# TensorE work in 64x64 tiles in a fused threshold attention and SoLU kernel

## The chip, the cores and the metric

The kernel runs on one core of one Trainium2 chip. Times are device microseconds (us) of one execution; medians are over four or more executions. Ratios are the mean time of one kernel's fast runs over the mean of the other kernel's fast runs of the same rounds, with a 95% interval, so they are not quite the ratio of the medians that stand beside them. A run over 1.5% above the fastest of its kernel is called slow and left out of ratios. The runs fall in five sessions (the changed kernel, e1 to e4, e5 to e8, e9 to e12, e13 to e15), each with runs of the kernel before beside them; its medians differ by up to 4.7 us between sessions, so I do not tell apart runs of different sessions that lie within some 5 us.

Engines are named as in the profile: PE is TensorE (PEld its weight loads), DVE VectorE, ACT ScalarE, POOL GpSimd, SP SyncE, which here issues transfers. A number such as L411 is a line of the kernel that ran.

## The reference

```python
# q, k, v: 8 batches x 8 heads x 576 tokens x 64, float32; tau = 0.02
scores = (1 / sqrt(64)) * q @ k.T
scores = where(scores >= max(scores) - tau, scores, -1e9)
attn   = exp(scores - max(scores));  attn /= sum(attn) + 1e-9
x      = (attn @ v) as (8*576, 8*64) = (4608, 512)        # tokens x (head, dim)
h      = x @ w_in                                         # 512 -> 1024
u      = h * softmax(h)
ln     = (u - mean(u)) / sqrt(var(u) + 1e-6) * g_ln
out    = ln @ w_out                                       # 1024 -> 512
```

`w_in` and `w_out` arrive as 64-bit floats and are converted on the chip in 16 pieces during the first 18 rounds; `g_ln` and the centring of `u` are folded into `w_out`.

## The kernel before

A pair is two heads of one batch, 64 dimensions each, on partitions 0 to 63 and 64 to 127. A round (one pass of the loop) takes one slot of attention: 128 tokens of both heads (a "last" slot holds the 64 left-over tokens of a pair as a block-diagonal query). Beside it the round does a quarter of a token tile of the feed-forward part: two rounds for `h_ps` (q0, q1), two for `o_ps` of the tile before (q2, q3). The whole kernel is software-pipelined by hand: what a round emits is what each engine has in its queue, in that order.

```python
    pairs_free = ["mm0", "mm1", "mm2"]      # three buffers of two PSUM banks: scores, h_ps
    banks_free = ["x0", "x1"]               # two single banks: transposes, pv, o_ps

    def scores(s):                          # 64x128 tiles: one head per row half
        ...
        for h, t, place in todo:
            tag, ps = take("s_ps")
            ...
            for ks in (slice(0, SM), slice(SM, S)):
                nc.tensor.matmul(out=ps[:, ks], lhsT=lhsT, rhs=kT[hh, ks], start=True, stop=True)

    def maxes(s):                           # VectorE: negated max, then nth = tau - max
    def exps(s):                            # ScalarE: Prelu as threshold (frees the banks), Exp with sum
    def normalise(s):
        nc.gpsimd.tensor_scalar(out=sm, in0=sm, scalar1=1e-9, scalar2=None, op0=ALU.add)
        nc.vector.reciprocal(out=sm, in_=sm)
        for x, w in enumerate(d["w"]):
            nc.gpsimd.tensor_scalar(out=w, in0=w, scalar1=d["sm"][:, x : x + 1], ...)
    def blocks(s):                          # VectorE transposes w in 32x32 blocks to T;
        ...                                 # SyncE issues 16 transfers per unit that sort T into wT
    def attend(key):                        # pv: 128x64 tiles, v against wT, five rounds later

    # the order in the loop of rounds
            scores(rnd); maxes(rnd)
            ...                             # attend, transposes, max and product of a token tile
            exps(rnd)
            if rnd - 1 >= 0 and rnd - 1 in live:
                normalise(rnd - 1)
            for job in late.pop(rnd, []):   # Exp of u, bn_stats, the rs chain, the output
                job()
            ...                             # h_ps or o_ps, then blocks(rnd - 1)
```

The loads of a batch are cut in twelve transfers, spread over rounds, on ScalarE's queue; the raw weights and the outputs are issued there too.

Of the kernel before, what the change touches and what calls it, by code (L numbers as in the profile page):

```python
# [20 lines left out]
def kernel(  # L21
# [23 lines left out]

    nc = tc.nc
# [8 lines left out]
    SCALE = 0.125  # L55

    const = ctx.enter_context(tc.tile_pool(name="const", bufs=1))
    loads = ctx.enter_context(tc.tile_pool(name="loads", bufs=2))
    heads = ctx.enter_context(tc.tile_pool(name="heads", bufs=5))
# [7 lines left out]
    mhalf = const.tile([P, 1], F32, name="mhalf")  # L67
    tau_t = const.tile([P, 1], F32, name="tau_t")
# [11 lines left out]
    NQE = 5  # L80
    q_ends = [const.tile([P, P], F32, name=f"q_end{x}") for x in range(NQE)]


    wTs = [const.tile([P, 5, 4, 160], F32, name=f"wT{x}") for x in range(2)]
    v_ends = [const.tile([P, H, D], F32, name=f"v_end{x}") for x in range(2)]

    batches = {}
    pairs = {}
    units = {}
    turned = 0  # L90
# [4 lines left out]
    pairs_free = ["mm0", "mm1", "mm2"]  # L95
    banks_free = ["x0", "x1"]
# [5 lines left out]
    def take_bank(name):  # L102
        tag = banks_free.pop(0)
        return tag, ps_mm.tile([P, 512], F32, tag=tag, name=name)


    def load(b):
        d = {}
        d["ends"] = ends = loads.tile([P, H, D], F32, tag="ends", bufs=1, name="ends")
        for nm in "qk":  # L110
            d[nm] = loads.tile([P, 4, H, D], F32, tag=nm, bufs=1, name=nm)
        d["v"] = loads.tile([P, H, 4, D], F32, tag="v", bufs=2, name="v")
        d["ve"] = v_ends[b % 2]
        batches[b] = d

        sides = (("q", q, slice(0, ST)), ("k", k, slice(ST, P)))
        if b == 0:

            for h in range(H):
                for (nm, src, side), queue in zip(sides, (nc.sync, nc.scalar if h < 2 else nc.sync)):  # L120
                    queue.dma_start(
                        out=d[nm][:, :, h], in_=src[b, h, 0:SM, :].rearrange("(p t) d -> p t d", t=4)
                    )
                    if h == 1:
                        queue.dma_start(
                            out=ends[side], in_=src[b, :, SM:S, :].rearrange("h p d -> p h d")
                        )
                if h == 1:
                    yield
        else:  # L130
            for nm, src, side in sides:
                for t in range(4):
                    nc.scalar.dma_start(
                        out=d[nm][:, t],
                        in_=src[b, :, 0:SM, :].rearrange("h (p t) d -> t p h d", t=4)[t],
                    )
                    if t % 2:
                        yield
                nc.scalar.dma_start(
                    out=ends[side], in_=src[b, :, SM:S, :].rearrange("h p d -> p h d")  # L140
                )
                yield
        queue = nc.scalar if b else nc.sync
        queue.dma_start(
            out=d["v"].rearrange("p h t d -> p h (t d)"),
            in_=v[b, :, 0:SM, :].rearrange("h (p t) d -> p h (t d)", t=4),
        )
        queue.dma_start(
            out=d["ve"][0:ST], in_=v[b, :, SM:S, :].rearrange("h p d -> p h d")
        )  # L150
        yield

    def constants():
# [4 lines left out]
        nc.gpsimd.memset(mhalf, -0.5)  # L158
        nc.gpsimd.memset(lim[:, 0:1], 1151.0)
        nc.gpsimd.memset(lim[:, 1:2], 255.0 * 8388608.0)  # L160
        for t in q_ends:
            nc.gpsimd.memset(t, 0.0)
        for t in v_ends:
            nc.gpsimd.memset(t[ST:P], 0.0)
        for t in wTs:
            nc.gpsimd.memset(t[ST:P, 4], 0.0)
# [11 lines left out]
        tag, g_ps = take_bank("g_ps")  # L178
# [4 lines left out]
        banks_free.append(tag)  # L183
# [12 lines left out]
    def weight_load(x):  # L196
        raw = work.tile([P, 512], I64 if wide else F32, tag=("xh2", "xh3")[x % 2], bufs=1, name="raw")
        nc.scalar.dma_start(out=raw, in_=piece(x)[0])
        raws[x] = dict(raw=raw)

    def weight_a(x):
# [4 lines left out]
        d["em"] = em = work.tile([P, 2, 512], I32, tag="em", bufs=1, name="em")  # L206
        e, m = em[:, 0], em[:, 1]
# [12 lines left out]
    def weight_b(x):  # L220
# [7 lines left out]
        e, m = d["em"][:, 0], d["em"][:, 1]  # L228
# [11 lines left out]
    def center():  # L240
        ones = work.tile([P, P], F32, tag="ob", name="ones")
        nc.vector.memset(ones, 1.0 / DFF)
        tag, mean = take_bank("mean")
        for c in range(NC):
            nc.tensor.matmul(out=mean, lhsT=ones, rhs=w2[:, c], start=c == 0, stop=c == NC - 1)
        for c in range(NC):
            nc.vector.tensor_tensor(out=w2[:, c], in0=w2[:, c], in1=mean, op=ALU.subtract)  # L247
        banks_free.append(tag)


    def prep(i, step):
        b, hp = divmod(i, NP)
        src = batches[b]
        two = slice(2 * hp, 2 * hp + 2)
        d = pairs.setdefault(i, {})
        tag, tp = take_bank("tp_" + "qke"[step])
        banks_free.append(tag)
        if step < 2:
            nm = "qk"[step]
            for t in range(4):  # L260
                nc.tensor.transpose(
                    out=tp[:, P * t : P * t + P], in_=src[nm][:, t, two],
                    identity=ident,
                )
            d[nm + "T"] = heads.tile([P, SM if step == 0 else S], F32, tag=nm + "T", name=nm + "T")
            if step == 0:
                nc.scalar.activation(out=d["qT"], in_=tp, func=AF.Copy, scale=scl)
            else:
                nc.scalar.copy(out=d["kT"][:, 0:SM], in_=tp)
            return  # L270
        nc.tensor.transpose(out=tp[:, 0:P], in_=src["ends"][:, two], identity=ident)
        for hh in (slice(0, D), slice(D, P)):
            nc.vector.tensor_scalar(
                out=q_ends[i % NQE][hh, hh], in0=tp[hh, 0:ST], scalar1=scl[hh], scalar2=None,
                op0=ALU.mult,
            )
        nc.vector.tensor_copy(out=d["kT"][:, SM:S], in_=tp[:, ST : 2 * ST])
        nonlocal turned
        turned += 1
# [3 lines left out]
    for b in range(B):  # L283
        for half in range(2):
            for hp in range(NP):
                for r in range(2 + half):
                    slots.append((b, half, hp, r))


    def tiles_of(half, r):  # L290
        if half == 0:
            return [(0, r, r), (1, r, 2 + r)]
        if r < 2:
            return [(0, 2 + r, r), (1, 2 + r, 3 + r)]
        return [(None, 4, 2)]
# [3 lines left out]
    def scores(s):  # L299
        b, half, hp, r = slots[s]  # L300
        i = b * NP + hp
        d = pairs[i]
        todo = tiles_of(half, r)
        qT, kT = d["qT"], d["kT"]
        made, tags = [], []
        for h, t, place in todo:
            tag, ps = take("s_ps")
            if h is None:
                hh, lhsT = slice(0, P), q_ends[i % NQE]
            else:  # L310
                hh = slice(D * h, D * h + D)
                lhsT = qT[hh, P * t : P * t + P]
            for ks in (slice(0, SM), slice(SM, S)):
                nc.tensor.matmul(out=ps[:, ks], lhsT=lhsT, rhs=kT[hh, ks], start=True, stop=True)  # L314
            made.append((ps, place))
            tags.append(tag)
        live[s] = dict(ps=made, tags=tags)

    def maxes(s):
        d = live[s]  # L320
        n = len(d["ps"])
        nm = small.tile([P, 2], F32, tag="nm", name="nm")
        for x, (ps, _) in enumerate(d["ps"]):
# [3 lines left out]
        nth = small.tile([P, 2], F32, tag="nth", name="nth")  # L327
        nc.vector.tensor_scalar(  # L328
            out=nth[:, 0:n], in0=nm[:, 0:n], scalar1=tau_t, scalar2=None, op0=ALU.add
        )  # L330
        d["nth"] = nth
# [3 lines left out]
    def exps(s):  # L335
        d = live[s]
        sm = small.tile([P, 2], F32, tag="sm", name="sm")
        d["w"] = []
        for x, (ps, _) in enumerate(d["ps"]):
# [6 lines left out]
        pairs_free.extend(d["tags"])  # L346
# [4 lines left out]
        d["sm"] = sm  # L351

    def normalise(s):
        d = live[s]
        n = len(d["w"])
        sm = d["sm"][:, 0:n]
        nc.gpsimd.tensor_scalar(out=sm, in0=sm, scalar1=1e-9, scalar2=None, op0=ALU.add)  # L357
        nc.vector.reciprocal(out=sm, in_=sm)  # L358
        for x, w in enumerate(d["w"]):
            nc.gpsimd.tensor_scalar(  # L360
                out=w, in0=w, scalar1=d["sm"][:, x : x + 1], scalar2=1.0, op0=ALU.mult,
                op1=ALU.mult,
            )

    n_units = 0

    def blocks(s):
        nonlocal n_units
        b, half, hp, r = slots[s]
        n = 4 + half  # L370
        key = (b, half, hp)
        if r == 0:
            units[key] = dict(T=work.tile([P, NB, n, 32], F32, tag="T", name="T"))
        T = units[key]["T"]
        d = live.pop(s)
# [308 lines left out]
```

## Time and profile before

| | before |
|---|---|
| median | 1123.45 us (1121.93 to 1125.1) |
| TensorE busy | 92% |
| VectorE, ScalarE, GpSimd busy | 63%, 52%, 28% |
| first `h_ps` starts, last scores end, end | 100.1, 1043.2, 1123.2 us |

The prediction below reads the page's busy shares, chain and groups. To them belong two more views. The first is the page's row for TensorE's granted clock over the span in 40 slices (9 is 90% or more). The second lists what TensorE waited for between 170 and 1044 us: the instruction that waited, what it waited for, us in total, times, longest.

```profile
PEclk9987799999998999999998999999998999999989
```

```profile
PE s_ps L314 <- ACT w L341: 12.5, 8, 2.6
PE pv L410 <- DMA wT<-T: 6.3, 6, 1.7
PE pv L410 <- ACT ob L517: 5.9, 10, 0.8
```

### The profile page before, as it was taken

The numbers are of one execution on the slowest core, as the hardware profiler recorded it, in microseconds if no ns is written. First come the engines' busy times: TensorE is split into PE (matmuls) and PEld (weight loads), VectorE is DVE, ScalarE is ACT, GpSimd is POOL, SyncE is SP. The second block draws the span as 40 slices with busy tenths as digits, with TensorE's granted clock in tenths as the row PEclk, the third lists the DMA queues.
The fourth block names the chain that finished last, engine by engine and source line by source line (L and its number), as shares of the span: only waits on it lengthen the run. The fifth ranks groups of instructions, "written<-read, shape, count | busy, mean of one in ns | idle before, by whom it ended". The sixth has DMA issues, their size and how long they took to land.

```text
span 1123.2 us, 15118 instructions
## 1 busy us (share of the span) xinstructions
PE 1029.3 (92%) x4817; PEld 555.8 (49%) x4817; DVE 711.3 (63%) x1401; ACT 581.2 (52%) x1170; POOL 309.9 (28%) x647
## 2 busy tenths in 40 slices
PE   6867789899999999999999999999999999999988
PEld 4433445445554555455544555445554555445533
DVE  3878866667656667766656667757656667766331
ACT  4656535555555556554555556555555556554211
POOL 2222212332223222332323222332223222432210
PEclk9987799999998999999998999999998999999989
DMA  7598424863467435763467435762467434444400
GB/s 173 140 188 218 109 53 105 170 143 71 108 144 166 104 82 117 167 147 71 107 150 156 104 82 116 170 144 66 110 144 163 103 85 102 98 103 95 94 10 28
DMA packets 259310, 132.11 MB, mean 118 GB/s; under 512 B 96920, under 2 KB 252576, under 8 KB 259232
## 3 DMA queue, kind: packets, MB, share of 16 engines
q1 hardware_dynamic: 173488, 88.15, 36.1%
q10 hardware_dynamic: 85744, 43.00, 15.4%
q8 instruction: 39, 0.64, 0.3%
q14 instruction: 39, 0.32, 0.1%
HBM read 36.70 MB, written 9.44 MB: 41 GB/s over the span
## 4 chain that ended last, share of the span: by engine, by line
PE 51%; DVE 18%; DMA 12%; ACT 6%; SPq 6%; POOL 3%; issue 3%; ACTq 0%; DVEq 0%
PE o_ps L510 15%; PE h_ps L446 13%; PE pv L410 11%; PE s_ps L314 9%; SPq L385 6%; DVE nm L324 5%; DVE T L377 5%; DMA wT<-T 5%; ACT w L341 3%; POOL w L360 3%; DMA v<-in_v_dram 3%; DVE u L465 2%; ACT w L348 2%; DMA q<-in_q_dram 1%; PE tp_u L497 1%
## 5 line engine op out<-in xcount | busy, mean ns | idle before, releaser
L360 POOL TENSOR_SCALAR w<-w,sm 128x576 f32<-128x576 f32 x288 | 211.6, 745 | 562.3 <-DVE sm L358 562.3
L377 DVE STREAM_TRANSPOSE T<-w 128x576 f32<-128x576 f32 x288 | 214.0, 771 | 134.2 <-POOL w L360 100.7
L324 DVE TENSOR_REDUCE nm<-s_ps 128x1 f32<-128x576 f32 x288 | 205.3, 748 | 118.5 <-PE s_ps L314 117.3
L341 ACT ACTIVATE w<-s_ps,nth 128x576 f32<-128x576 f32 x288 | 199.5, 740 | 142.8 <-DVE nth L328 99.0
L510 PE MATMUL o_ps<-w,uT 128*128 128x512 f32 x576 | 263.1, 601 | 5.1 <-DVE w L247 3.5
L314 PE MATMUL s_ps<-kT,qT 64*128 64x512 f32 (+1 forms) x1024 | 218.9, 472 | 39.8 <-ACT w L341 31.6
L446 PE MATMUL h_ps<-w,xh 128*128 128x512 f32 x512 | 239.8, 613 | 0.3 <-ACT w L341 0.3
L348 ACT ACTIVATE w<-w,ntau 128x576 f32<-128x576 f32 x288 | 220.7, 774 | 1.0
L314 PEld LDWEIGHTS s_ps<-kT,qT 64*128 64x128 f32 x1024 | 120.0, 198 | 182.3 <-issue 101.2
L410 PE MATMUL pv<-wT,v 128*64 128x192 f32 (+2 forms) x1536 | 159.2, 348 | 16.6 <-DMA wT<-T 7.0
L510 PEld LDWEIGHTS o_ps<-w,uT 128*128 128x128 f32 x576 | 105.3, 192 | 120.1 <-issue 113.1
L446 PEld LDWEIGHTS h_ps<-w,xh 128*128 128x128 f32 x512 | 95.0, 196 | 104.7 <-issue 103.6
L410 PEld LDWEIGHTS pv<-wT,v 128*64 128x64 f32 x1536 | 108.2, 143 | 44.9 <-issue 19.6
L357 POOL TENSOR_SCALAR sm<-sm 128x2 f32<-128x2 f32 (+1 forms) x160 | 39.0, 243 | 158.5 <-ACT w L348 154.5
L425 ACT COPY xh<-pv 128x256 f32<-128x256 f32 x32 | 11.9, 371 | 108.6 <-PE pv L410 108.6
L497 PE MATMUL tp_u<-ident,u 128*128 128x128 f32 x288 | 45.6, 282 | 13.5 <-ACT ob L517 4.7
L348 ACT ACTIVATION_READ_ACCUMULATOR w<-w,ntau 128x1 f32 x288 | 57.1, 198 | 0.0
L421 ACT COPY xh<-pv 128x256 f32<-128x256 f32 x32 | 11.9, 372 | 86.8 <-PE pv L410 75.0
L410 PE MATMUL pv<-wT,v_end 128*64 128x256 f32 (+2 forms) x384 | 52.8, 336 | 0.0
L459 ACT ACTIVATE u<-h_ps,hm 128x1024 f32<-128x1024 f32 x36 | 39.8, 1105 | 25.1 <-DVE hm L453 25.1
L453 DVE TENSOR_REDUCE hm<-h_ps 128x1 f32<-128x1024 f32 x36 | 43.9, 1219 | 11.9 <-PE h_ps L446 11.7
L500 ACT COPY uT<-tp_u 128x512 f32<-128x512 f32 x36 | 21.0, 585 | 57.7 <-PE tp_u L497 56.0
(65 smaller groups left out, 704.9 us busy)
## 6 DMA issues: line engine op xcount, KB each, us to landing
wT<-T SPq DMA_DIRECT2D x512, 80.0 KB, 2.2
wT<-T SPq DMA_DIRECT2D x256, 100.0 KB, 2.3
wT<-T SPq DMA_DIRECT2D x256, 64.0 KB, 2.1
out_dram<-ob ACTq DMA_DIRECT2D x32, 256.0 KB, 2.6
q<-in_q_dram ACTq DMA_DIRECT2D x28, 256.0 KB, 4.7
k<-in_k_dram ACTq DMA_DIRECT2D x28, 256.0 KB, 4.6
v<-in_v_dram ACTq DMA_DIRECT2D x7, 1024.0 KB, 6.8
raw<-in_moe_w_in_dram ACTq DMA_DIRECT2D x8, 512.0 KB, 4.8
```

The lines of the kernel that those rows point to most:

```text
L314: nc.tensor.matmul(out=ps[:, ks], lhsT=lhsT, rhs=kT[hh, ks], start=True, stop=True)
L324: nc.vector.tensor_reduce(out=nm[:, x : x + 1], in_=ps[:, 0:S], axis=AX.X, op=ALU.max, negate=True)
L341: nc.scalar.activation(out=w, in_=ps[:, 0:S], func=AF.Prelu, bias=d["nth"][:, x : x + 1], scale=1.0, alpha=1.0e30,)
L348: nc.scalar.activation(out=w, in_=w, func=AF.Exp, bias=ntau, scale=1.0, accum_out=sm[:, x : x + 1])
L360: nc.gpsimd.tensor_scalar(out=w, in0=w, scalar1=d["sm"][:, x : x + 1], scalar2=1.0, op0=ALU.mult, op1=ALU.mult,)
L377: nc.vector.transpose(out=T[:, :, place, :], in_=w)
L385: nc.sync.dma_start(out=wT[32 * c : 32 * c + 32, 0:nj, a, 0 : 32 * n], in_=T[32 * a : 32 * a + 32, c : NB : 4].rearrange("p j t q -> p j ( ...
L410: nc.tensor.matmul(out=to[:, a0:a1, 0 : 32 * n], lhsT=vv, rhs=wT[:, c, a0:a1, 32 * first : 32 * first + 32 * n], start=c == 0, stop=c == 4,)
L446: nc.tensor.matmul(out=h[:, f], lhsT=x[:, c], rhs=w1[:, c, f], start=c == 0, stop=c == NP - 1)
L453: nc.vector.tensor_reduce(out=d["nm"], in_=d["h"], axis=AX.X, op=ALU.max, negate=True)
L497: nc.tensor.transpose(out=tp[:, P * c : P * c + P], in_=d["u"][:, x : x + P], identity=ident)
L510: nc.tensor.matmul(out=d["o"], lhsT=d["uT"][:, c], rhs=w2[:, c], start=c == 0, stop=c == NC - 1)
```

## The change

The intent is to make every TensorE instruction in the steady part a 64x64 tile, so that none has to wait at a change of shape until the array has drained, and so that four run at once. To get there the change also

- puts the last tokens of two pairs in one slot (18 slots per batch instead of 20), 
- does the transposes as 64x64 products into the spare columns of the scores' banks, which leaves the scores one pair of buffers (`s0`, `s1`) and `pv`, `h_ps` and `o_ps` another two (`p0`, `p1`),
- sets a GpSimd memset ("fence") between the two parts of a product in which the row halves exchange banks,
- moves `normalise` behind the token tile's `late` jobs, with the reciprocal as a power on GpSimd,
- attends four rounds later instead of five, and moves raw weights and outputs to SyncE's queue and gathers the loads of a batch, still on ScalarE's queue, into ten transfers issued in four rounds.

The core of the diff, with cuts marked; the comments are added here.

```diff
+    def fence(first):
+        m = nc.gpsimd.memset(mark, 0.0)
+        for mm in first:
+            sync(m, mm)
+        return m
...
-        nc.scalar.dma_start(out=raw, in_=piece(x)[0])
+        nc.sync.dma_start(out=raw, in_=piece(x)[0])
...
+    def turn(spare, x, lhsT_of):            # a transpose as four 64x64 products
+        o = spare["base"] + 64 * x
+        to = slice(o, o + 64)
+        for r in range(2):
+            for y in range(2):
+                nc.tensor.matmul(
+                    out=spare[r][ROWS[y], to], lhsT=lhsT_of(r, y), rhs=ident[ROWS[r], ROWS[r]], ...)
...
+    def scores(s, items):
+        ps = [ps_mm.tile([P, 1024], F32, tag=f"s{h}", name="s_ps") for h in range(2)]
+        spare = dict(enumerate(ps), base=S)
+        for n, make, keep in items:         # transposes of q, k, ends or u
+            make(spare, x)
+            ...
+        for ks in (slice(SM, S), slice(0, SM)):
+            for h in range(2):
+                for y in range(2):
+                    ...                     # 64x64 tiles
+        for keep, x in kept:                # ScalarE copies from s0, VectorE from s1
+            keep(spare, x)
...
-        nc.vector.reciprocal(out=sm, in_=sm)
+        nc.gpsimd.tensor_tensor(out=sm, in0=sm, in1=mone, op=ALU.pow)
...
+        for c in range(NP):                 # ff_h; ff_o and attend alike
+            for r in range(2):
+                f = slice(512 * (part ^ r), 512 * (part ^ r) + 512)
+                for y in range(2):
+                    mm = nc.tensor.matmul(
+                        out=h[ROWS[y], f], lhsT=x[ROWS[r], c, ROWS[y]], rhs=w1[ROWS[r], c, f], ...)
+                    if part and not last:
+                        sync(mm, d["fence"])
...
-    LAG_PV = 5
+    LAG_PV = 4
...
-            if rnd - 1 >= 0 and rnd - 1 in live:
-                normalise(rnd - 1)
             for job in late.pop(rnd, []):
                 job()
+            if rnd - 1 in live:
+                normalise(rnd - 1)
```

## The prediction

> **What bounds the kernel now.** I read the busy shares first, then the chain that ended last, then the costliest groups, and last the timeline of TensorE in a few microseconds of the steady part.
>
> ```profile
> PE 1029.3 (92%) x4817; PEld 555.8 (49%) x4817; DVE 711.3 (63%) x1401; ACT 581.2 (52%) x1170; POOL 309.9 (28%) x647
> PE 51%; DVE 18%; DMA 12%; ACT 6%; SPq 6%; POOL 3%; issue 3%; ACTq 0%; DVEq 0%
> L377 DVE STREAM_TRANSPOSE T<-w 128x576 f32<-128x576 f32 x288 | 214.0, 771 | 134.2 <-POOL w L360 100.7
> L324 DVE TENSOR_REDUCE nm<-s_ps 128x1 f32<-128x576 f32 x288 | 205.3, 748 | 118.5 <-PE s_ps L314 117.3
> L341 ACT ACTIVATE w<-s_ps,nth 128x576 f32<-128x576 f32 x288 | 199.5, 740 | 142.8 <-DVE nth L328 99.0
> L360 POOL TENSOR_SCALAR w<-w,sm 128x576 f32<-128x576 f32 x288 | 211.6, 745 | 562.3 <-DVE sm L358 562.3
> L485 POOL TENSOR_TENSOR rs<-rs,mhalf 128x1 f32<-128x1 f32 x36 | 20.4, 567 | 3.0
> ```
>
> TensorE is the bound: 92% busy, first in the chain, and VectorE, next, has 37% to spare. The groups below TensorE wait for it or for each other. So what matters is whether TensorE's busy time is work. The timeline, with start and length in us ahead of each group:
>
> ```profile
> 500.87 1.19 PE L314 MATMUL s_ps<-kT,q_end 128*128 128x512 f32 x4
> ...
> 505.78 0.60 PE L497 MATMUL tp_u<-ident,u 128*128 128x128 f32 x4
> 506.31 1.30 PE L314 MATMUL s_ps<-kT,qT 64*128 64x512 f32 x8
> 507.54 0.33 PE L271 MATMUL tp_e<-ident,ends 128*128 128x128 f32 x1
> ...
> 1050.08 1.52 PE L410 MATMUL pv<-wT,v 128*64 128x192 f32 x16
> ```
>
> Each fp32 product is two matmul records, and one record of N columns streams for 2N cycles: consecutive h_ps records (N = 512) start 428 ns apart, 1024 cycles at 2.4 GHz. Eight 64-row records of two heads take 1.30 us, little more than four full ones (1.19 us): the two row halves **already run side by side**. Likewise sixteen 64-column pv records would need 16 x 160 ns = 2.56 us in series and take 1.52. So tiling has no factor of two left. What it can save is around changes of shape. Records of equal shape follow each other without loss; at a change I find a gap of 0.13 to 0.22 us and a first record 50 to 105 ns longer than its successors. I counted 309 changes (128x128, 64x128, 128x64), gaps under 1 us summing to 47 us; with some 80 ns for each first record, **about 72 us** of the span.
>
> **What the Trainium skill says.** "TensorEngine Tiling (Array Packing)", section Tiling Modes, says a change of tiling mode drains TensorE while tiles of one mode work independently; the gaps and the overlapping heads agree. The same page, Restrictions and Gotchas, says that different row tiles may not use one PSUM bank at once and software must order them: hence the fences; nothing in this trace tests it. "TensorE: Matmul & The Clock Gate", Part 3, gives 10.6 times for 16 concurrent tiles, so four should overlap; the trace shows only two. Its Part 1 says that an idle window of some 3.4 us halves the clock; here the clock falls to half for 6.8 us at 339, 592 and 844 us, so such idle time occurs every two batches.
>
> **The change part by part.** I call one slot of the loop a round; four rounds (two of h_ps, two of o_ps, named q0 to q3) make one token tile.
>
> *TensorE work.* One 64x64 matmul of N columns costs its own tile 4N cycles, and four tiles overlap. Scores: 576 x 4 cycles = 0.96 us per slot as before, but a batch has 18 slots instead of 20, because two pairs' last tokens share one instead of a block-diagonal query being half zeros: 2 x 0.96 = 1.9 us per batch, 15 us in all. h_ps or o_ps: 3.41 us per round, unchanged. A 128x128 transpose costs 107 ns, as 108 now. PV of a unit costs two parts of 5 x 128 x 4 cycles, 1.07 us each, the same sum as before. Instruction count grows about fourfold; where pv had just waited for a semaphore, four TensorE instructions came in 36 ns (494.56 to 494.60 us), so I expect no limit from issue.
>
> A cycle of four rounds is then: q0 and q1 each 0.43 (transposes of u) + 0.96 + 1.07 + 3.41 + 1.07 = 6.94 us; q2 0.43 + 0.96 + 3.41 = 4.80; q3 0.54 + 0.96 + 3.41 = 4.91. Sum **23.6 us**, or 106 us per batch of 4.5 cycles. Before, a batch takes half of 680.0 - 427.3 us (first h_ps two batches apart), 126.4 us. If TensorE never waited, the gain would be 20 us x 8 = 160 us.
>
> *What takes it back.* Scores now have one pair of buffers, s0 and s1, so scores of the next round (and the transposes that share those buffers) must wait until Prelu has read this round's. Also the normalisation on GpSimd is now emitted behind the statistics of the token tile, and its reciprocal is a GpSimd power. Follow q3, with 0 where TensorE has streamed its scores: max starts at 0.2 and takes 1.42 for two, nth until 1.88, u's product (1.22) until 3.1, two bn_stats (1.29) and aggregate (0.21) until 4.6. GpSimd, waiting for it, does four small rs operations (335, 220, 567, 191 ns with 0.09 between) until 6.25, then the sum's add 0.24, power (**my estimate 0.75**, from 567 ns for one column), and the first w (0.745): 8.25. VectorE's in-order queue holds T of the round before: 8.3 to 9.8; a copy of u's transposes (0.42, between 0.22 for 64 columns and 0.67 for 512) until 10.1; only now q0's max, until 11.5; nth 11.7; two Prelus on ScalarE until 13.2; TensorE restarts at 13.4. TensorE, from 0: o_ps 3.41, q0's transposes and scores after q3's Prelu (3.5) until 5.0, then 1.07 + 3.41 + 1.07 until about 10.6. It **stands idle for some 2.8 us**. From 13.4: 0.43 + 0.96 + 1.07 + 3.43 + 1.07 = 20.4, q2 0.43 + 0.96 + 3.43 = 25.2, q3 0.54 + 0.96: **26.8 us** per cycle. Other rounds have slack: q1's Prelu ends at 18.2, before TensorE needs it at 20.4; q2's ends at 25.1 against 25.2.
>
> *Fences.* 127 memsets of about 0.1 us. Each lies 3.4 us or a round ahead of its user, so it should be free; the tightest is q0's PV, behind the delayed normalisation (9.05 against a need at 9.6).
>
> *Other engines.* VectorE loses 196 reciprocals of 0.155 us (30 us) and gains 32 pairs x two copies of 0.42 us (27 us) less 18 us of q_end: near 700 us. GpSimd gains 144 x 0.75 + 36 x 0.57 + 127 x 0.1 = 141 us: about 450. ScalarE loses a little. DMA of w has longer contiguous rows; it is hidden anyway.
>
> *Sum.* Start to the first h_ps: 100.1 us before, bound by VectorE and converting weights; now 12 rounds for 13: 93. Scores end at round 144, so 132 rounds: 32 cycles with h_ps x 26.8 = 858, four rounds without it (no new tile is ready twice) 22, weights still converting in rounds 12 to 16, 6. Tail: from the end of scores the old one takes 80 us (1043 to 1123); the new has 4 h_ps and 5 o_ps tiles of 6.84, transposes and PV 7, output and small waits 13: 82. 93 + 858 + 22 + 6 + 82 = **1061**; I put 1058.
>
> **The rivals.** (a) *TensorE stays the bound and gets nearly all drains back.* If the stall is hidden, as it would be if GpSimd's chain were 2.8 us shorter, 1061 - 32 x 2.8 = 970. For: VectorE's load per cycle is only about 18.5 us of 23.6. Against: the in-order queues above. (b) *VectorE's and GpSimd's latency bounds*, my main case. Each microsecond mis-sized in the chain costs 32 us; a power of 1.2 us makes 1075. (c) *Four small tiles overlap badly, or issue bounds.* The 64-column transposes need an instruction every 13 ns. If weights or issue double PV and transposes, a cycle gains some 6 us: 1240. For: fourfold instructions, and only pairs of tiles are seen overlapping. Against: 64-column score records already follow at 55 ns with two tiles. (d) *Fences held in GpSimd's queue* reach TensorE; one more us each cycle makes 1090.
>
> **Range and chances.** 1058, and 1000 to 1115 eight times in ten: the lower edge is two thirds of the stall hidden, the upper 1.8 us more per cycle. Within 2% needs over 1100.7. Faster 0.80, within 2% 0.12, slower 0.08; the last is rival (c).
>
> **What would show it.** Shape changes gone except in the tail, and 144 slots. Scores' matmuls of four tiles starting within some 40 ns, and h_ps at 3.4 us a part. Waits: TensorE on Prelu (scores' buffers) some 2 to 3 us once a cycle, at u's transposes; VectorE's T waiting for GpSimd's w over 3 us once a cycle; few waits of TensorE on the memset. TensorE's start-to-start of cycles near 26.8 us. I am wrong if cycles are under 25 (stall hidden), or if PV parts take well over 1.1 us each (issue), or if TensorE waits on fences. The least certain terms are the power's length and the overlap of four tiles.

## The result and the profile after

The changed kernel is slower: 1241.53 us median (1236.49 to 1255.22, four runs) against 1123.45 us (1121.93 to 1125.1). The ratio of the fast runs is 1.1036 [1.0998, 1.1074]; the run of 1255.22 us is slow and left out. The prediction said 1058 us and gave slower 0.08.

The page of the changed kernel, which answers to the lines of before: busy shares, clock, and the groups of the chain that the prediction followed. (Its chain of what ended last breaks off at the last instruction and is not read.)

```profile
PE 987.8 (80%) x18569; PEld 684.5 (55%) x18569; DVE 682.3 (55%) x1164; ACT 576.3 (47%) x1241; POOL 442.0 (36%) x930
PEclk7566769898889989899999998999999999999999
L411 ACT ACTIVATE w<-s_ps,nth 128x576 f32<-128x576 f32 x288 | 197.7, 738 | 350.6 <-DVE nth L401 258.1
L439 DVE STREAM_TRANSPOSE T<-w 128x576 f32<-128x576 f32 x288 | 210.7, 764 | 174.7 <-POOL w L427 130.6
L425 POOL TENSOR_TENSOR sm<-sm,mone 128x2 f32<-128x2 f32 x144 | 104.2, 724 | 12.0
```

Busy TensorE time fell by 41.5 us, and VectorE's by 29 us, but the span grew by 111.5 us: no engine is over 80%. ScalarE stands idle 350.6 us in front of Prelu (L411) instead of 142.8. The clock row has a 5 and 6s at the start and more 8s later. What TensorE waited for between 206 and 1144 us:

```profile
PE s_ps L264 <- ACT w L411: 55.8, 64, 4.0
PE h_ps L554 <- ACT ob L673: 30.1, 8, 5.7
PE s_ps L264 <- DVE u L579: 24.7, 24, 3.9
PE o_ps L658 <- ACT xh L520: 10.9, 5, 5.0
PE pv L491 <- POOL mark L106: 5.9, 2, 3.0
```

L264 are the transposes that open a round's use of `s0` and `s1`. They wait 64 times for Prelu, which reads the scores of the round before: that is the wait the prediction named. The second and fourth entries it did not name: ScalarE comes late with an output or a copy of `pv`.

The next four blocks of lines are one stall, the timelines of four engines around the last round of a token tile (q3) and the first of the next (q0). Start and length in us stand ahead; in brackets are the idle time before and what ended it.

TensorE:

```profile
608.68 0.88 PE L264 MATMUL s_ps<-ident,u 64*64 64x64 f32 x30 [0.79 <-DVE u L579]
...
609.40 1.19 PE L385 MATMUL s_ps<-kT,qT 64*64 64x64 f32 x14
...
611.51 3.60 PE L554 MATMUL h_ps<-w,xh 64*64 64x512 f32 x30
...
618.50 0.33 PE L264 MATMUL s_ps<-ident,u 64*64 64x64 f32 x4 [2.29 <-ACT w L411]
...
619.60 2.18 PE L385 MATMUL s_ps<-kT,qT 64*64 64x64 f32 x14
```

VectorE:

```profile
605.72 1.42 DVE L397 TENSOR_REDUCE nm<-s_ps 128x1 f32<-128x576 f32 x2 [0.69 <-ACT qe L335]
...
613.86 1.50 DVE L439 STREAM_TRANSPOSE T<-w 128x576 f32<-128x576 f32 x2 [3.77 <-DMA wT<-T]
615.29 0.38 DVE L617 COPY uT<-s_ps 128x256 f32<-128x256 f32 x1
615.60 1.40 DVE L397 TENSOR_REDUCE nm<-s_ps 128x1 f32<-128x576 f32 x2
```

GpSimd:

```profile
612.26 0.72 POOL L425 TENSOR_TENSOR sm<-sm,mone 128x2 f32<-128x2 f32 x1
613.08 1.48 POOL L427 TENSOR_SCALAR w<-w,sm 128x576 f32<-128x576 f32 x2
```

ScalarE:

```profile
617.71 1.37 ACT L411 ACTIVATE w<-s_ps,nth 128x576 f32<-128x576 f32 x2 [6.48 <-POOL mark L106]
```

Read from the bottom up. TensorE restarts at 618.50, as soon as the first Prelu of 617.71 has read `s0`. Prelu waited for `nth`, and so for q0's max (615.60; the profile names the fence's memset, which ended at about the same time). The max stands in VectorE's queue behind T (613.86), which waited 3.77 us. The profile puts that wait down to a transfer, but T starts when the first of GpSimd's two products, begun at 613.08, is done: that is the power and the delayed normalisation. So far it is the predicted chain, with an idle time of 2.29 us where 2.8 were predicted. Two things are new. q3's max started only at 605.72, some 1.3 us after its scores had streamed, behind two copies out of the score banks and a wait of 0.69 us for ScalarE's copy `qe`. And after the stall fourteen score records take 2.18 us, where those of the round before took 1.19: the clock is at half for some 3.4 us.

To size this I added up, from TensorE's records that start between 180 and 980 us, the gaps under 1 us at changes of shape, all other gaps, and the time at half clock, which costs at most half of itself. A record of N columns is taken to end when its 2N cycles have streamed (428 ns for N = 512, twice that at half clock), so that slow streaming does not count as a gap; gaps count from 20 ns.

| us in 800 | changes of shape, gaps | other gaps | at half clock |
|---|---|---|---|
| before | 246, 34.7 | 59.2 | 23.9 |
| changed | 1, 0 | 143.1 | 94.9 |

The drains are gone, as intended: some 35 us gained. 83.9 us more of other gaps, and up to 35.5 us of clock, took their place.

### The profile page after: what moved, and what is told of

It is laid out like the page before. It is cut to its first block, busy times and chain, and to the rows that moved or that the text cites. A ratio compares the mean times of both kernels' runs of the same rounds, so it can differ in the third digit from the quotient of the medians.

```text
span 1234.7 us, 43204 instructions
## 1 busy us (share of the span) xinstructions
PE 987.8 (80%) x18569; PEld 684.5 (55%) x18569; DVE 682.3 (55%) x1164; ACT 576.3 (47%) x1241; POOL 442.0 (36%) x930
## 5 line engine op out<-in xcount | busy, mean ns | idle before, releaser
L411 ACT ACTIVATE w<-s_ps,nth 128x576 f32<-128x576 f32 x288 | 197.7, 738 | 350.6 <-DVE nth L401 258.1
L554 PE MATMUL h_ps<-w,xh 64*64 64x512 f32 x1856 | 233.6, 623 | 38.0 <-ACT ob L673 30.1
L658 PE MATMUL o_ps<-w,uT 64*64 64x256 f32 x3968 | 233.6, 379 | 11.5 <-ACT xh L520 10.9
L397 DVE TENSOR_REDUCE nm<-s_ps 128x1 f32<-128x576 f32 x288 | 203.9, 749 | 62.2 <-ACT qe L335 24.2
L658 PEld LDWEIGHTS o_ps<-w,uT 64*64 64x64 f32 x3968 | 193.6, 134 | 63.0 <-ACT xh L520 18.9
L491 PEld LDWEIGHTS pv<-wT,v 64*64 64x64 f32 x4096 | 175.6, 143 | 79.6 <-issue 39.8
L491 PE MATMUL pv<-wT,v 64*64 64x128 f32 x4096 | 191.5, 288 | 11.0 <-POOL mark L106 6.9
L385 PE MATMUL s_ps<-kT,qT 64*64 64x64 f32 (+1 forms) x2048 | 184.5, 453 | 19.5 <-ACT w L411 19.1
L554 PEld LDWEIGHTS h_ps<-w,xh 64*64 64x64 f32 x1856 | 106.9, 142 | 118.5 <-issue 68.6
L264 PE MATMUL s_ps<-ident,u 64*64 64x64 f32 x1984 | 63.3, 243 | 83.5 <-ACT w L411 49.5
L264 PEld LDWEIGHTS s_ps<-ident,u 64*64 64x64 f32 x1984 | 51.4, 149 | 107.9 <-ACT w L411 100.3
L425 POOL TENSOR_TENSOR sm<-sm,mone 128x2 f32<-128x2 f32 x144 | 104.2, 724 | 12.0
L385 PEld LDWEIGHTS s_ps<-kT,qT 64*64 64x64 f32 x2048 | 61.2, 148 | 23.3 <-ACT w L411 21.9
L617 DVE COPY uT<-s_ps 128x256 f32<-128x256 f32 x62 | 25.1, 405 | 88.0 <-PE s_ps L385 88.0
L264 PE MATMUL s_ps<-ident,k 64*64 64x64 f32 x992 | 32.0, 239 | 36.1 <-ACT w L411 36.1
```

What stands on the lines that cost most here:

```text
L264: nc.tensor.matmul(out=spare[r][ROWS[y], to], lhsT=lhsT_of(r, y), rhs=ident[ROWS[r], ROWS[r]], start=True, stop=True,)
L385: nc.tensor.matmul(out=ps[h][ROWS[y], ks], lhsT=lhsT, rhs=d["kT"][ROWS[h], ks], start=True, stop=True,)
L397: nc.vector.tensor_reduce(out=nm[:, x : x + 1], in_=ps[:, 0:S], axis=AX.X, op=ALU.max, negate=True)
L411: nc.scalar.activation(out=w, in_=ps[:, 0:S], func=AF.Prelu, bias=d["nth"][:, x : x + 1], scale=1.0, alpha=1.0e30,)
L425: nc.gpsimd.tensor_tensor(out=sm, in0=sm, in1=mone, op=ALU.pow)
L491: mm = nc.tensor.matmul(out=y[ROWS[h], 512 * u : 512 * u + P].rearrange("p (a x) -> p a x", a=4), lhsT=ve[ROWS[r], h0 + h] if j == 4 else ...
```

## The experiments

All are edits of the changed kernel and all gave correct results. I write "loads" for q, k, v of the batches after the first. The runs of before beside them had medians of 1124.8 to 1128.1 us. My theory at first was that the delayed normalisation and ScalarE's queue make the waits; the rivals were the tiling itself, the fences, and SyncE's queue.

**e1_norm_first: the normalisation back ahead of the `late` jobs.**

```diff
+            if rnd - 1 in live:
+                normalise(rnd - 1)
             for job in late.pop(rnd, []):
                 job()
-            if rnd - 1 in live:
-                normalise(rnd - 1)
```

> The normalisation is emitted ahead of the token tile's statistics again, as in the kernel before; nothing else changes. Theory: the 9.9 us round (q3 to q0) is the GpSimd chain of small rs operations ahead of the normalisation, on which VectorE's T and then q0's max wait; T could start 3.7 us earlier, TensorE then waits only for its own work, so 2 to 2.8 us less in each of 33 cycles: about 1165 us (1150 to 1185), and VectorE's wait for GpSimd's w falls from 131 us to under 50. Rival: other waits (ScalarE's blocked queue, u's product) stand right behind and take the time: 1205 to 1240 us.

Measured: 1170.47 us, ratio 1.0401 [1.0343, 1.0459]; 71 us of the 118 are back. The step from q3 to q0 went from 9.9 to 6.5 us in a typical cycle. A step is the time from the first Prelu of a round to that of the next, the median of the steady cycles. The order of one call is the largest single part.

**e2_loads_sp: the loads on SyncE's queue.**

```diff
-                nc.scalar.dma_start(     # q and k
+                nc.sync.dma_start(
...
-                queue = nc.scalar        # ends, and likewise v
+                queue = nc.sync
```

> All loads of later batches are issued by SyncE instead of ScalarE; nothing else changes. Theory: ScalarE stands up to 6 us at a load's issue behind earlier transfers, and holds back the copies that free the buffers of h_ps and o_ps; the waits of h_ps on ob (30 us) and of o_ps on xh (11 us) vanish: about 1200 us. Rival: the load's wait moves to SyncE, delays the transfers of w there, and PV waits instead: within 1% of 1241 us.

Measured: 1207.06 us, ratio 1.0721 [1.0671, 1.0771], 34.5 us less. The changed kernel shows why. ScalarE's timeline (ACTq is the issue of a transfer), and TensorE's:

```profile
671.27 0.40 ACTq L128 DMA_DIRECT2D q<-in_q_dram  x1
...
674.63 0.41 ACTq L128 DMA_DIRECT2D k<-in_k_dram  x1
675.08 0.69 ACT L673 ACTIVATE ob<-o_ps,rs 128x512 f32<-128x512 f32 x1 [2.35 <-DMA wT<-T]
```

```profile
675.82 3.66 PE L554 MATMUL h_ps<-w,xh 64*64 64x512 f32 x32 [1.89 <-ACT ob L673]
```

The issue of k's load waits for almost 3 us in ScalarE's queue; the output `ob` behind it frees the buffer that `h_ps` needs. Before, twelve issues were spread over rounds, and `h_ps` did not share its buffers with `o_ps`.

**e3_norm_loads: both.** The edit is the sum of the two.

> Both edits. Theory: the two waits lie in different rounds and add: some 1120 to 1140 us, and the clock's half-speed stretches in the steady part fall below half of the 27 there were. Rival: the larger of the two alone, 1165 us.

Measured: 1130.57 us, ratio 1.0042 [0.9996, 1.0088]: the same as before. The effects add (71 + 34.5 = 105.5, together 111). With these two moves undone and the tiling kept, the kernel is as fast as before.

**e4_ff128: `h_ps` and `o_ps` in 128x128 tiles, without their fences.**

```diff
-                ff_h(cur, 0, rnd + 1 < NS)
+                ff_h(cur, 0, False)
...
-        if not d["osplit"]:
+        if True:                          # o_ps too, in the same buffer
```

> h_ps and o_ps as 128x128 matmuls without fences, all else in 64x64 tiles. It brings back two changes of shape in each of about 128 rounds and takes away 63 fences. If the drains still counted in full, 128 x 2 x 0.2 = 51 us more: 1290 us. If TensorE is not the bound in most rounds (my theory: it waits some 4 us per cycle), the drains fall partly into its waits: 1245 to 1275 us. If four tiles at once or the fences were the loss (rival c or d), it is faster than 1241 by 20 us or more.

Measured: 1235.88 us, ratio 1.0971 [1.093, 1.1013]. That is below the range of my theory: drains return (200 changes of shape and 29.6 us of gaps between 180 and 980 us), and the time does not move. Other gaps fall from 143.1 to 109.1 us: the drains lie in time in which TensorE would have waited. Its largest wait between 206 and 1144 us is that of the changed kernel; the one for u is smaller (24.7 us there), and that of `h_ps` for `ob` falls from 30.1 to 5.9 us:

```profile
PE s_ps L264 <- ACT w L411: 54.9, 57, 2.6
PE s_ps L264 <- DVE u L579: 16.6, 22, 3.4
```

**e5_weights_act: e3, with the raw weights on ScalarE's queue.**

```diff
-        nc.sync.dma_start(out=raw, in_=piece(x)[0])
+        nc.scalar.dma_start(out=raw, in_=piece(x)[0])
```

> On top of e3: the 16 loads of raw weights are issued by ScalarE again, as in the kernel before. Theory: on SyncE each stood behind 16 issues of w's transfers at 0.6 us, so that VectorE waited 35 us for raw weights, ScalarE 57 us for VectorE, and every second round of the first 16 took 11 to 15 us. The first 18 rounds should take 155 to 165 us instead of 190: 1130 becomes 1095 to 1105 us, later batches unchanged. Rival: the slow start comes from the single pair of score buffers and the conversion itself: 1120 to 1130 us.

Measured: 1095.37 us, ratio 0.9714 [0.9654, 0.9775]; 35 us less, all in the first 18 rounds, which take 152.4 us instead of 190. SyncE is busy for three quarters of the time with the 16 transfers of each unit, as its own timeline of the changed kernel shows (one line is one burst of issues):

```profile
666.02 11.35 SPq L449 DMA_DIRECT2D wT<-T  x16
```

That is 0.71 us per issue; a unit comes every 15 us (nine in a batch of some 137 us), and what is queued behind a burst waits for it. In e3 the first conversion of a piece waits 5.66 us for its raw weights at 46.57 us, and TensorE 9.25 us at 51.48 us behind it.

**e6_copies_early: e5, with the copies out of the score banks ahead of the 512-column scores.** This tests whether the copies can be taken off VectorE's path to max.

```diff
         for ks in (slice(SM, S), slice(0, SM)):
+            if ks.start == 0:
+                for keep, x in kept:
+                    keep(spare, x)
...
-        for keep, x in kept:
-            keep(spare, x)
```

> On top of e5: the copies of the transposes out of the scores' banks are emitted between the 64-column and the 512-column scores instead of after both. Theory: they now wait for the last score matmul and come ahead of max in VectorE's queue, so that each round's chain is 0.4 to 0.7 us longer; beside the 512-column matmuls they should cost nothing: 20 to 35 us less than e5. Rival: TensorE's own 23.6 us per cycle covers them: within 0.5% of e5. Third: TensorE waits for the copies before the 512-column scores: slower than e5 by 20 us or more.

Measured: 1221.98 us, ratio 1.0839 [1.0774, 1.0905], 127 us more than e5. TensorE's waits over the whole run:

```profile
PE s_ps L388 <- ACT qe L335: 64.3, 31, 5.5
PE s_ps L388 <- ACT uT L618: 51.2, 62, 5.5
PE s_ps L388 <- ACT qT L295: 38.4, 31, 6.0
```

The scores now wait for the copies. By the code the two are in different banks of one tile (the 512-column scores fill the first, the copies read the second), so the program orders them by tile; a finer order was not tried. In both orders that were tried the copies cost time: they stand either ahead of max or ahead of the scores.

**e7_lag5: e5, attending five rounds later again.**

```diff
-    LAG_PV = 4
+    LAG_PV = 5
```

> On top of e5: PV follows its last scores by five rounds instead of four. Theory: a 12 us round once or twice per two batches in e3 is PV waiting for w's transfers, delayed on SyncE by the loads; with a round more they have landed: 15 to 30 us less than e5. Rival: the later PV delays the token tiles and the tail by a round or two: within 0.5%, or slower.

Measured: 1080.48 us, ratio 0.9594 [0.9528, 0.9661], 15 us less than e5. `pv` had waited 17.2 us for transfers of wT between 180 and 990 us in e5; in e7 that entry is gone. What TensorE still waits for most, between 180 and 980 us:

```profile
PE s_ps L264 <- DVE u L579: 29.5, 26, 3.8
PE s_ps L264 <- ACT w L411: 11.0, 26, 3.1
```

**e8_loads_pool: e3, with the loads on GpSimd's queue instead of SyncE's.** The edit is e2's with `nc.gpsimd`.

> As e3, but the loads of later batches are issued by GpSimd instead of SyncE. Theory: neither ScalarE nor SyncE is held up; GpSimd has half its time free: 1110 to 1125 us against 1130. Rival: a load that waits for earlier transfers holds up GpSimd's normalisation and fences just as it held up ScalarE: 1145 to 1170 us.

Measured: 1129.25 us, ratio 1.0019 [0.9946, 1.0093], no different from e3 and between the two ranges that I gave. What mattered was that ScalarE was rid of them; whether they stand among SyncE's bursts or apart from them made no measurable difference.

**e9_max_order: the changed kernel, max of `s1` ahead of `s0`**, so that VectorE need not wait at once for ScalarE's copy out of `s0`.

```diff
-        for x, ps in enumerate(d["ps"]):
+        for x, ps in reversed(list(enumerate(d["ps"]))):
             nc.vector.tensor_reduce(...)
```

> The changed kernel with one edit: of the two maxes of a round, the one over s1 comes first. The max over s0 waits for ScalarE's copy out of the same bank, which stands behind ScalarE's Exp of u (0.65 to 1.2 us in q2 and q3); s1 was copied by VectorE itself, so its max can use that time. Theory: q3's max opens the chain that ends in TensorE's stall, so each cycle gains about 0.7 us: 1241 becomes 1215 to 1222 us. Rival: ScalarE's blocked queue or TensorE hides it: within 0.5%.

Measured: 1228.24 us, ratio 1.0886 [1.0821, 1.0951]; 13 us less, the direction expected and some half of the size. In the changed kernel max had waited 24.2 us for `qe` and 16.4 us for `qT`; part of that time is not on the path.

**e10_lag5_max_order: e7 and e9 together.**

> e7 (normalisation first, loads on SyncE, weights on ScalarE, lag 5) with the order of maxes of e9. TensorE still waits for u's product some 1 us per cycle, and the product stands behind q3's max: 15 to 25 us less than e7's 1080. Rival: the wait moves to Prelu: within 0.5% of 1080.

Measured: 1071.65 us, ratio 0.9511 [0.9463, 0.9559]; 9 us less than e7, again less than expected.

**e11_lag5_ff128: e7 with e4's 128x128 `h_ps` and `o_ps`.** With the waits away, the drains ought to show.

> e7 with h_ps and o_ps as 128x128 matmuls without fences. In e4 the drains vanished in TensorE's waits; here TensorE is busy nearly all the time, so two changes of shape of 0.2 us in 128 rounds should now show: 1080 becomes 1115 to 1130 us. Rival: the 64x64 form is worth nothing here either (1075 to 1090), and all that e7 gains over the kernel before comes from scores and order.

Measured: 1076.53 us, ratio 0.9555 [0.9499, 0.961]. My expectation missed: 238 changes of shape with 37.4 us of gaps are back, and the time is that of e7 or a little less. Other gaps fell from 64.9 to 32.3 us, and the time at half clock from 30.7 to 6.8.

**e12_max_order_recip: e10 with VectorE's reciprocal in place of GpSimd's power for the sums.**

```diff
-        nc.gpsimd.tensor_tensor(out=sm, in0=sm, in1=mone, op=ALU.pow)
+        nc.vector.reciprocal(out=sm, in_=sm)
```

> e10 with the reciprocal of the sums on VectorE instead of GpSimd's power (0.72 us). With the normalisation ahead of the statistics the power is off the path: within 0.7% of e10. If GpSimd's chain still bounds, 10 us or more faster; if VectorE does, 10 us or more slower.

Measured: 1074.05 us, ratio 0.9536 [0.9468, 0.9603], the same as e10. With the normalisation ahead of `late`, the power is off the path.

By here the waits were named, but not why the prediction, which had the late normalisation in it, came out 183 us low. The next two runs bear on that, and the last looks for the best mixture.

**e13_chain_alone: e7, with the changed kernel's own order (normalisation behind `late`).** It keeps the predicted chain and nothing of the moved queues; it also attends five rounds later, where the prediction had four.

> e7 with the changed kernel's own order on GpSimd (normalisation behind the statistics): loads on SyncE, weights on ScalarE, lag 5. This is what the prediction's chain assumed. If the chain was sized right (26.8 us per cycle), about 1065 us plus a few; if copies out of the scores' banks ahead of max and the clock's half-speed after each stall add what they seem to in e2 (29 us per cycle), 1150 to 1170 us.

Measured: 1180.35 us, ratio 1.0441 [1.0376, 1.0505]: 100 us more than e7, 122 more than the prediction, and above both ranges that I gave. Between 180 and 1070 us TensorE waits for what the prediction said and for u:

```profile
PE s_ps L264 <- ACT w L411: 71.4, 77, 3.1
PE s_ps L264 <- DVE u L579: 21.6, 24, 3.8
```

**e14_chain_recip: e13 with VectorE's reciprocal.** The edit is e12's.

> e13 with VectorE's reciprocal (0.155 us) in place of GpSimd's power (0.72 us). The power stands in the chain that stalls TensorE: if the chain bounds once per cycle, about 0.5 us less in each of 33 cycles, 12 to 20 us faster than e13. Rival: the reciprocal itself waits in VectorE's queue behind other work: within 0.5% of e13.

Measured: 1167.94 us, ratio 1.0324 [1.0249, 1.0399]; 12.4 us less. Here the power is on the path: the step from q3 to q0 goes from 9.9 to 9.2 us.

**e15_max_order_ff128: e10 with 128x128 `h_ps` and `o_ps`.**

> e10 with h_ps and o_ps as 128x128 matmuls without fences. In e11 the returning drains (37 us of gaps) took the place of other gaps and of half-speed clock. Theory: rounds are set by VectorE and ScalarE, so the same here: within 1% of e10's 1072. If TensorE is the bound in e10, 20 us or more slower.

Measured: 1062.16 us (1060.25 to 1064.12), ratio 0.9393 [0.9336, 0.9451]: the fastest of all, 6% ahead of the kernel before. It keeps 64x64 tiles for scores, transposes and `pv`, the merged slots and the fences of `pv`, and drops the 64x64 form for the feed-forward products. Its page, and what TensorE waits for between 180 and 980 us:

```profile
PE 962.8 (91%) x13561; PEld 525.2 (50%) x13561; DVE 680.9 (64%) x1164; ACT 578.9 (55%) x1241; POOL 437.7 (41%) x867
PEclk8577879999899999999999999999999999999999
```

```profile
PE s_ps L264 <- ACT w L411: 6.4, 6, 3.1
PE s_ps L264 <- DVE u L579: 3.5, 1, 3.5
```

Waits on Prelu are down from e13's 71.4 us in 890 to 6.4 us in 800, and after the start every slice but one has its full clock. What is left of the change's gain is not taken apart: no run undoes the merged slots, or the 64x64 form of scores, transposes and `pv`. The rounds did not become shorter: 6.3 us before (126.4 us for 20 slots), 6.6 in e7 (118.5 for 18). So fewer rounds per batch may be the larger part of it.

## Why the prediction was wrong

The prediction's sum had three terms. I set them beside the same three in the traces: when the first `h_ps` starts, from there to the last scores, and the tail. The sums are the spans of the profiled runs.

| us | predicted | e13, chain alone | changed | e15 |
|---|---|---|---|---|
| to the first `h_ps` | 93 | 111.5 | 123.6 | 106.1 |
| to the end of the last scores | 886 | 972.7 | 1019.0 | 855.5 |
| tail | 82 | 96.9 | 92.1 | 96.8 |
| sum | 1061 | 1181.1 | 1234.7 | 1058.4 |

The changed kernel misses by some 61 us of queues (1241.5 - 1180.4, medians), which the prediction left out, and by some 120 us in the terms that it did work out: 87 in the middle, 18 at the start, 15 in the tail. Part of the last two is e13's later attention: in e5, which attends four rounds later as predicted, the first `h_ps` starts at 103.3 us and the tail is 90.2, against 112.8 and 95.3 in e7. Step by step:

- **The stall: the mechanism right, the size with some luck.** "stands idle for some 2.8 us" from the late normalisation: the idle time of the stall shown is 2.29 us, the step from q3 to q0 is 9.9 us in a typical cycle against 9.85 in its working. Errors cancel in this: max starts 1.1 us late in both rounds, TensorE is done with its work 11.8 us after q3's scores instead of 10.6, and TensorE restarts after the first Prelu, where the working waits for both. Taking the stall away is worth 99.9 us (e13 against e7), or 3.0 us for each of 33 cycles; rival (a) gave 90 us for it. But that holds the clock too: half clock falls from 88.7 us in 800 to 30.7. On the changed kernel itself the same move gave 71 us (e1). VectorE's T did wait for over 3 us once a cycle, and "my estimate 0.75" for the power measured 0.724 us.
- **The cycle without the stall: wrong, and the term that was mis-sized.** "Other rounds have slack" is the step that failed; for q2 that slack was 0.1 us ("25.1 against 25.2"). With it "Sum **23.6 us**" has TensorE wait nowhere but in the stall, and at full clock. e7 has no such stall, and its batches take 118.5 us, or 26.3 us per cycle of four rounds. Between 180 and 980 us it has 64.9 us of gaps and 30.7 us at half clock: over 30.4 cycles that is 2.1 us and at most 0.5 us per cycle, which is nearly all of the 2.7. Its largest waits there, shown with e7, are for u's product and for Prelu, each about once in a cycle. Add the stall, and e13's 29.7 us per cycle stands against 26.8; times 32 cycles it is 93 us, near the 87 above. Its typical steps show which rounds: q2 to q3 took 6.3 us instead of 5.0, q0 to q1 6.1 instead of 4.95, q1 to q2 7.7 instead of 7.0.
- **"max starts at 0.2": wrong.** The copies out of the score banks wait for the last score matmul and stand ahead of max in VectorE's queue; the shown stall has 0.42 + 0.21 us of them and 0.69 us of waiting for ScalarE's, so max starts at about 1.3. I had them beside the scores. u's product then ends 4.1 us after the scores instead of 3.1, later than `o_ps` ("3.41"), and u's transposes wait 0.79 us. The Trainium skill's "PSUM — Partial Sum Buffer", section Terms, says that two engines on one bank and quarter of the partitions at once is an error, reads against reads included; max and the copy `qe` read columns of one bank, and the wait of 0.69 us between these two readers is what keeping them apart costs here. e9 shows 13 us of it directly.
- **"here the clock falls to half for 6.8 us": seen, and not carried over.** The idle window of 3.4 us that it cites was taken for the length of the idle time ("so such idle time occurs"); the gaps at 339, 591 and 844 us are of 2.62 us. The prediction noted the half clock before and then used full speed for the new cycle. The changed kernel has 94.9 us of half clock in 800, e13 88.7. What share of the lost time is clock and what share is copies no run separates: clock changes only with the gaps that cause it.
- **"If TensorE never waited, the gain would be 20 us x 8 = 160 us"; drains of "about 72 us": counted right, worth nothing for `h_ps` and `o_ps`.** All drains are gone in the changed kernel, and e4 puts 200 back for the same time (5.6 us less, within noise). e11 and e15 put 238 and 240 back; e11 is the same as e7 within noise (4 us less), and e15 is 10 us faster than e10. In these runs other gaps shrank by as much as the drains put back. For scores, transposes and `pv` no run puts the drains back.
- **The start: wrong by 31 us.** "now 12 rounds for 13: 93" took rounds to cost what they did. With raw weights behind SyncE's bursts they cost more; e5 returns 35 us over the first 18 rounds. Even e15 needs 106.1 us.
- **Queues: not looked at.** The diff showed weights and outputs changing queue and loads gathered into four rounds, and the prediction has not a word on it beyond "DMA of w ... is hidden anyway". Loads cost 34.5 us, weights 35 us, the shorter lag 15 us, each measured with other edits around it: together they are 84.5, but e13, with the normalisation late, is only 61 us faster than the changed kernel. For the issuing engine, the Trainium skill's "DMA: Bandwidth & Descriptors", section Issuing engines are not separate DMA queues, says that spreading the issues only saves the sequencer's time, "usually small relative to the DMA itself". Here 16 issues took 11.35 us of SyncE, and which engine issued was worth 35 us twice.
- **Fences and overlap: right.** Rival (d) did not come: TensorE waited for a fence twice in 938 us, 5.9 us in all. Rival (c) did not come either: a part of `h_ps` in four tiles took 3.60 us to its last record, but the next work starts 3.43 us after it, and one of `pv` took about 1.2 us against 1.07 worked out. Slower came true, but not by rival (c), for which its chance stood: it was rival (b), latency, at several times the size that it was given.

Open: 15 us of tail; why 128x128 `h_ps` and `o_ps` are 10 us *faster* in e15 (waits for u's product are 3.5 us there and 15.8 us in e10, but I have not shown why); which drains the scores' and `pv`'s tiles save and what the merged slots are worth; and what the issue of k's load waits for in ScalarE's queue, which the profile puts down to a transfer of wT.

## What to carry to other kernels

A change that removes drains, or any small loss, gains little where the bound engine then waits: before counting the gain, follow the round's dependencies once more with every copy and every in-order queue in it, and start max where the last copy ends, not where the scores end. Treat a moved call or a moved transfer in a diff as a change of its own with its own cost: here one moved call and one moved group of loads made 111 of the 118 us that the new kernel lost, and the tiling of `h_ps` and `o_ps` none that shows; the other tiling was not tried apart. And when a waiting kernel's cause is named, try the parts of the change apart: the best kernel kept some of them and dropped others.

## What the Trainium skill lacked or had wrong

- "TensorE: Matmul & The Clock Gate", Part 1 and the table at its end, has the clock fall after an idle window of some 3.4 us and advises against gaps over some 3 us. Here shorter single gaps were followed by half clock: 2.29 us (changed kernel, 618.50 us), 19 of 22 gaps of 1.96 to 2.26 us in e13, and 1.51 us in e7 and e15 (249.7 and 239.2 us). Others were not: 2.34 us in the changed kernel (904.4 us), 2.43 us in e13 (341.4 us). So the runs give no fixed length. Its section on a second failure mode tells of short idle times that do this, also without a length.
- "TensorEngine Tiling (Array Packing)", Tiling Modes, says that a change of mode drains TensorE, without a size. Before, a change took a gap of 0.13 to 0.22 us and a first record 50 to 105 ns longer; 200 to 240 of them put back (e4, e11, e15) cost no time that shows, beside waits.
- No page has the throughput of four 64x64 tiles in fp32: from the start of a part of `h_ps` to that of the next work it took 3.43 us in 32 records of 512 columns, and 3.44 us before in eight of 128x128 (medians at full clock).
- "DMA: Bandwidth & Descriptors", Issuing engines are not separate DMA queues, calls the issuer's time usually small. A burst of 16 issues on SyncE took 11.35 us, 0.71 us each, against about 2 us from issue to landing.
- "GPSIMD Engine Reference" has no time for a power: 0.57 us for 128x1 and 0.72 us for 128x2, against 0.158 us for VectorE's reciprocal of 128x2.
